# Joins, loads, an activation, two sums and the last store set at other places in a fused attention and MLP kernel

## The chip, the cores and the metric

The kernel runs on one core of one Trainium2 chip. The metric is device microseconds of one execution; before the change the median of three runs is 606.25 us (605.91 to 606.29). Lower is better.

## The reference

Two blocks follow each other. The first is a linear attention with a decaying state, for 4 batches of 8 heads, 768 tokens, head size 48; the second an MLP of 384 to 2048 to 384 on the 3072 tokens, gated with the error function of softplus.

```python
for t in range(S):
    kt, vt, rt, wt = (k[:, :, t], v[:, :, t], r[:, :, t], w[:, :, t])
    cur = np.einsum('bhd,bhe->bhde', u[None] * kt, vt)
    y[:, :, t] = np.einsum('bhd,bhde->bhe', rt, state + cur)
    state = wt[:, :, :, None] * state + np.einsum('bhd,bhe->bhde', kt, vt)
...
h = x @ w_in
sp = np.maximum(h, 0.0) + np.log1p(np.exp(-np.abs(h)))
g = h * erf(sp)
return (g @ w_out).astype(np.float32)
```

The MLP weights are given in float64. The kernel reads them as pairs of 32-bit words and makes float32 of them on the chip.

## The kernel before

**Steps.** The work is cut into 12 steps (n_steps): a chunk of 128 tokens of two of the four batches each. Step s does the attention of its chunk, and beside it the hidden layer (`hidden`, L963) of step s-1 and the output projection (`project`, L1013, from step 3 on `project_fast`, L1089) of step s-3. What runs when is written out by hand: each engine executes its instructions in the order of the program (`tc.manual_schedule`), and generators (`hidden`, `project`, `prepare`) are advanced piece by piece from `attend`.

**Attention, steps 1 to 4 (`attend`, L853).** A chunk is treated in blocks of doubling length, levels 1 to 6 (LOG). A level has products on TensorE (`level_products`, L527, into the PSUM tiles pp), a scaling of the r and k tile `in` in place on VectorE (`scale`, L302, L325), and a copy of the products that count into the tile `own` (`take_level`, L543: a masked copy, L547, or on ScalarE, L554). Step 0 (`attend_first`, L728) has an order of its own. After each level `attend` calls `early(level - 1)` ahead of the masked copy, `next(following)` behind it, and then `place(level - 1)`, which sends stages of the weight conversion (`convert_at`), activations (`advance`) and pieces of hidden layer or projection (`beside`). At the end, `through_state` (L583) adds what the state carries and copies the result to `xT`; in step 0 the last part of it is a function, `hop`, called inside step 1's first level.

**Step preparation (`prepare`, L351).** For the next step it makes the products of decay factors on GpSimd (L399). Steps from 4 on get their first 3 or 4 levels another way, the near products: terms for each distance between tokens (`term`, L457, on VectorE for short and on GpSimd for long distances), summed by VectorE (`sum_up`, L448, L450). Terms share two tiles: those of distances 0 and 4 are overwritten by those from 9 on. From step 4's preparation of step 5 on, distances go up to 15.

**Weight conversion (`convert`, L213).** The weights come in 16 pairs of column groups: 0 to 7 of w_in, 8 to 15 of w_out. A pair passes the stages l (load of its words, 2 transfers of 384 KB on SyncE's queue, three buffers), b (high word scaled on ScalarE, L245 or L247), r (low word scaled on ScalarE, L253, two buffers shared with the row loads), and j (join): h on VectorE (L262, for w_out also L267) and o, an integer addition on GpSimd (L275). The table CONVERT (L1222) says for steps 1 to 3 which stages are sent at which level; of each entry the first string is sent by `early`, the second by `place`. Before, pair 13's join is sent at level 1 of step 3, pair 14's at level 2 and pair 15's at level 3, each in the second string. The hidden layer of step 0 uses pairs 0 to 7 one by one during step 1 (one piece a level), its projection uses pairs 8 to 15 during step 3 (two pieces a level).

**Loads.** All transfers in question are issued by SyncE, in program order, and a transfer that waits holds up those behind it. `load(i, behind=x)` first copies one element of x into the buffer's first element, so the transfer waits for x. In step 0 pairs 2, 3 and 4 are loaded behind `own`; `load_step(2)` and `load_v(2)` follow in step 1 at level 2. The v transfer waits until the state products of step 0 (`pending`, L827) have been done.

**Activations.** A hidden half of 8 column groups is copied from PSUM (L1005), and then passes softplus (L978), erf (L981), each with a table load on ScalarE, and a multiplication on VectorE (L985). The list STAGES (L1229) says how many of these `advance` sends at each level of steps 1 to 3.

**The end.** `project_fast` makes the two 128-row outputs o of a step from seven products of half width. In the last step its last part (L1127 to L1132) is split into the right half (hi) and the left half (lo): the right half is added and stored ahead of the product for the left half.

Of the kernel before, what the change touches and what calls it, by code (L numbers as in the profile page):

```python
# [11 lines left out]
FP32 = mybir.dt.float32  # L12
# [5 lines left out]
P = 128  # L18
# [4 lines left out]
NJ = 2  # L23
# [16 lines left out]
DIRECT = 4  # L40
NEAR_LOG = 4
NEAR = 1 << NEAR_LOG
LOG = 6
# [18 lines left out]
def kernel(  # L62
# [14 lines left out]
    nc = tc.nc  # L77
# [8 lines left out]
    KT = DM // P  # L86
# [81 lines left out]
    def load_second(behind):  # L168
# [6 lines left out]
        load_halves(t, rkw[1])  # L175

    def load_v(s):

        vt = loaded[s][1]
        nc.sync.dma_start(out=vt[:], in_=v[s])  # L180

    def load_step(s):
        t = ins.tile([P, 2, JP, C], FP32, name="in")
        vt = ins.tile([P, NH, D], FP32, name="v")
        if s < DIRECT:
            load_halves(t, rkw[s])
        else:
            nc.sync.dma_start(out=t[:], in_=rkw[s][:, 0:2])
        if 2 < s <= DIRECT:
            load_w(s)  # L190
        if s == 3:
            nc.sync.dma_start(out=block_sb[:], in_=block_mask)
            nc.sync.dma_start(out=u_row[:], in_=u_rows)
        loaded[s] = t, vt
        if s > 2:
            load_v(s)

# [15 lines left out]
    def convert(weights):  # L213
# [6 lines left out]

        def load(i, behind=None):
            if i >= len(weights):
                return
            dst, src = weights[i]
            if plain:
                nc.sync.dma_start(out=dst, in_=src)
                return
            words = wide.tile([P, 2, DM, 2], I32, name="words", bufs=3)
            if behind is not None:
                nc.gpsimd.tensor_copy(out=words[:, 0, 0, 0:1].bitcast(FP32), in_=behind)  # L230
            load_halves(words[:].rearrange("p i n two -> p i (n two)"), src.bitcast(I32))
            held[i] = {"words": words}
# [118 lines left out]
    def prepare(s):  # L351
# [123 lines left out]
        else:  # L475
# [4 lines left out]
            term(nc.gpsimd, 5, 6, 7, 8)  # L480
            nc.vector.tensor_mul(terms[0], terms[0], r)
            sum_up(0, 4)
            term(nc.gpsimd, *range(9, NEAR))
# [99 lines left out]
    def through_state(s, xT):  # L583
# [20 lines left out]
        if not s:  # L604
            parts = y[:, 0, :, 0], y[:, 0, :, 1], y[:, 1, :, 0]

            def hop():
# [6 lines left out]
                for kk in range(KT):  # L614
                    nc.scalar.copy(by_kk[kk], parts[kk])

            turns["hop"] = hop
# [110 lines left out]
    def attend_first(xT):  # L728
# [76 lines left out]
        stages["l"](2, own[:, 0, HC // 2 : HC // 2 + 1])  # L805
        stages["l"](3)
        stages["b"](1, 0)
# [7 lines left out]
        stages["r"](1)  # L815
        stages["l"](4)
        stages["h"](1)
# [35 lines left out]
    def attend(s, xT, early, place, behind):  # L853
# [11 lines left out]
        for level in range(near_log(s) + 1 if s == DIRECT else 1, LOG + 1):  # L865
# [14 lines left out]
            if s == 1 and level == 2:  # L880
                turns.pop("pending")()
                load_step(2)
                load_v(2)
            if s != 1 or level < LOG:
# [6 lines left out]
            else:  # L891
                take_level(own, pp, level)
            if level > 1 and (s, level) != (DIRECT, LOG - 1):
                next(following, None)
            if s == 2 and level == 1:
# [4 lines left out]

                turns["ahead"] = ahead
            place(level - 1)

        from_own(s, own, 1)
# [184 lines left out]
    def project_fast(s, gs):  # L1089
# [36 lines left out]
        yield  # L1126
        parts = (hi, lo) if s == n_steps - 1 else (slice(0, DM),)  # L1127
        for part in parts:
            if part is parts[-1]:
                product(m1[:, lo], a12, b21, True)  # L1130
            nc.vector.tensor_add(o[0][:, part], o[0][:, part], m1[:, part])  # L1131
            nc.sync.dma_start(out=out[i * NJ, c, :, part], in_=o[0][:, part])  # L1132
        yield
# [60 lines left out]
    def run_late(s, tokens, following=None):  # L1194
# [30 lines left out]
        (("", "jbrl"),) * 4 + (("", "jl"), ("", ""), ("", ""), ("", ""), ("", "br")),  # L1225
        (("", "jbr"), ("", "jbr"), ("", "j")),
    )
# [19 lines left out]
    with tc.manual_schedule(  # L1247
# [15 lines left out]
        for s in range(n_steps):  # L1263
# [7 lines left out]
            def place(n):  # L1271
# [7 lines left out]
                if s in ALONE:  # L1279
                    if s == 2 and not n:  # L1280

                        next(hids[0])
                        turns.pop("ahead")()
                    convert_at(n)
                    advance(STAGES[s][n])
                else:
# [129 lines left out]
```

## Time and profile before

| what | us |
|---|---|
| median of 3 runs (lowest, highest) | 606.25 (605.91, 606.29) |
| the profiled execution | 604.11 |
| its span, first to last instruction | 602.3 |
| TensorE (PE) busy, matmuls | 584.2 (97%) |
| VectorE (DVE) busy | 436.8 (73%) |
| ScalarE (ACT) busy | 361.5 (60%) |
| GpSimd (POOL) busy | 272.5 (45%) |

Times in the timeline count from the start of the span. TensorE's clock is the share of full speed that the throttle granted, 0.994 over the span. A line such as "PE a <- POOL b: 6.5, 1, 6.5" says that TensorE's instructions a waited for GpSimd's b: 6.5 us in all, once, 6.5 at the longest; "issue" stands where the profile shows nothing that was waited for. In a timeline line stand the start, the busy time, the engine, the source line, the operation, what it writes and reads, the count, and in brackets the idle time ahead of it with its releaser. The 12 steps do not look alike: step 0 ends near 29 us, step 1 near 62, step 2 near 97, step 3 near 158, step 4 near 208, and from there a step takes 44.5 us, in which TensorE is hardly ever idle.

### The profile page before, as it was taken

The page shows a single profiled execution, that of the slowest core. Times are in us where ns is not written, and L with a number is a line of the kernel's source. Part 1 is how long each engine was busy: PE and PEld are TensorE (multiplying, and loading weights), DVE is VectorE, ACT ScalarE, POOL GpSimd, SP SyncE. Part 2 cuts the span into 40 slices and gives each one's busy share as a digit, 9 for nine tenths or more (in the row PEclk, how much of TensorE's full clock was granted, in tenths as well). Part 3 has the DMA queues.
Part 4 walks back from the last instruction along what each step waited for, and adds up shares of the span by engine and source line. Part 5 has one row for each costly group of instructions (what it writes and reads, how often), then busy time and mean ns, then how long its engine had stood idle before and what let it go on. Part 6 is the DMA issues. An engine that isn't in the chain of part 4 may idle for free.

```text
span 602.3 us, 16616 instructions
## 1 busy us (share of the span) xinstructions
PE 584.2 (97%) x7264; PEld 500.6 (83%) x7264; DVE 436.8 (73%) x519; ACT 361.5 (60%) x473; POOL 272.5 (45%) x305
## 2 busy tenths in 40 slices
PE   8889999969999999999999999999999999999997
PEld 6678787548758857899899898898898898898996
DVE  6666884979897699799799799799799624023140
ACT  4548867607435298675864765765765664746710
POOL 3546382520569739829639539549549100000000
PEclk9999999979999999999999999999999999999999
DMA  7964572313224334324334334333331300000000
GB/s 238 315 220 162 207 252 81 139 55 104 67 90 153 73 102 159 80 103 170 71 106 168 71 106 167 72 106 132 72 106 53 72 8 27 2 21 13 2 28 26
DMA packets 54081, 63.24 MB, mean 105 GB/s; under 512 B 35160, under 2 KB 40568, under 8 KB 52984
## 3 DMA queue, kind: packets, MB, share of 16 engines
q1 hardware_dynamic: 53624, 61.98, 32.3%
q8 instruction: 57, 0.93, 0.6%
q10 hardware_dynamic: 384, 0.20, 0.1%
q14 instruction: 16, 0.13, 0.1%
HBM read 52.39 MB, written 8.69 MB: 101 GB/s over the span
## 4 chain that ended last, share of the span: by engine, by line
PE 81%; DVE 8%; ACT 6%; issue 3%; POOL 1%; ACTq 1%; DVEq 0%; POOLq 0%
PE m L996 39%; PE m L1104 27%; PE pp L535 5%; PE m L1028 3%; PE y L569 2%; PE pp L641 2%; DVE in L325 1%; PE y L595 1%; PE m L839 1%; DVE words L464 1%; DVE rk L460 1%; DVE h L985 1%; ACT room L952 1%; PE pp L907 1%; DVE own L547 1%
## 5 line engine op out<-in xcount | busy, mean ns | idle before, releaser
L996 PE MATMUL m<-xT,w_in_sb 128*128 128x256 f32 x1152 | 256.7, 381 | 1.2 <-ACT h L1005 1.2
L996 PEld LDWEIGHTS m<-xT,w_in_sb 128*128 128x128 f32 x1152 | 216.3, 190 | 31.8 <-ACT h L1005 1.3
L1005 ACT COPY h<-m 128x512 f32<-128x512 f32 x96 | 55.5, 579 | 85.9 <-PE m L996 85.8
L325 DVE TENSOR_TENSOR in<-in,tot_sb 128x1024 f32<-128x1024 f32 (+1 forms) x59 | 79.7, 1351 | 25.1 <-PE pp L535 22.1
L460 POOL TENSOR_TENSOR rk<-words 128x528 f32<-128x528 f32 (+3 forms) x28 | 41.6, 1487 | 91.7 <-DVE sums L450 81.3
L464 POOL TENSOR_TENSOR words<-words,rest 128x528 f32<-128x528 f32 (+10 forms) x77 | 79.0, 1026 | 6.0
L1028 PE MATMUL m<-w_out_sb,h 128*128 128x384 f32 x192 | 66.5, 502 | 6.5 <-POOL w_out_sb L275 6.5
L1028 PEld LDWEIGHTS m<-w_out_sb,h 128*128 128x128 f32 x192 | 36.6, 195 | 31.4 <-POOL w_out_sb L275 7.1
L1104 PE MATMUL m<-w_out_sb,h 128*128 128x192 f32 x288 | 50.4, 329 | 1.0 <-DVE o L1131 1.0
L1104 PE MATMUL m<-mixed,h 128*128 128x192 f32 x288 | 51.1, 331 | 0.0
L1104 PEld LDWEIGHTS m<-w_out_sb,h 128*128 128x128 f32 x288 | 46.9, 190 | 1.8 <-DVE o L1131 1.3
L952 ACT ACT_TABLE_LOAD x36 | 46.2, 1283 | 2.7 <-issue 2.1
L1104 PEld LDWEIGHTS m<-mixed,h 128*128 128x128 f32 x288 | 46.6, 190 | 0.9
L956 ACT ACT_TABLE_LOAD x36 | 46.2, 1283 | 1.6 <-DVE room L1087 1.1
L1104 PE MATMUL m<-w_out_sb,room 128*128 128x192 f32 x256 | 44.2, 326 | 0.0
L535 PEld LDWEIGHTS pp<-in 48*64 48x64 f32 (+1 forms) x2368 | 33.5, 126 | 11.7 <-issue 6.7
L1104 PEld LDWEIGHTS m<-w_out_sb,room 128*128 128x128 f32 x256 | 42.0, 190 | 0.0
L961 DVE TENSOR_TENSOR h<-h,y 128x1024 f32<-128x1024 f32 x17 | 20.7, 1215 | 28.3 <-ACT y L956 28.2
L535 PE MATMUL pp<-in 48*64 48x64 f32 (+1 forms) x2368 | 38.0, 212 | 1.2 <-DVE in L325 1.1
L952 ACT ACTIVATE room<-h 128x1024 f32<-128x1024 f32 x36 | 38.1, 1057 | 0.4
L961 DVE TENSOR_TENSOR h<-h,pp 128x1024 f32<-128x1024 f32 x19 | 23.1, 1214 | 19.6 <-ACT pp L956 19.6
L460 POOL TENSOR_TENSOR words<-words 128x336 f32<-128x336 f32 (+6 forms) x49 | 35.3, 720 | 3.8
(140 smaller groups left out, 820.8 us busy)
## 6 DMA issues: line engine op xcount, KB each, us to landing
in<-in_rkw SPq DMA_DIRECT2D x8, 1024.0 KB, 5.4
words<-in_moe_w_in SPq DMA_DIRECT2D x16, 384.0 KB, 5.1
words<-in_moe_w_out SPq DMA_DIRECT2D x16, 384.0 KB, 4.0
words<-in_rk_rows SPq DMA_DIRECT2D x8, 768.0 KB, 5.9
w<-in_rkw SPq DMA_DIRECT2D x11, 512.0 KB, 6.6
v<-in_v SPq DMA_DIRECT2D x12, 384.0 KB, 5.8
out<-o SPq DMA_DIRECT2D x23, 192.0 KB, 2.7
in<-in_rkw SPq DMA_DIRECT2D x7, 512.0 KB, 6.1
```

What stands on the lines that cost most here:

```text
L325: nc.vector.tensor_mul(halves, halves, view(tots[level - 1], 0, [[1, n], [2, nb], [0, half]]))
L460: engine.tensor_mul(terms[n], r[:, :, n:], k[:, :, : near - n])
L464: engine.tensor_mul(k[:, :, :m], k[:, :, :m], w[:, :, n : n + m])
L535: nc.tensor.matmul(pp[s0 : s0 + m, e, n, :m], lhsT=rk[rows(e), 1, n, s0 : s0 + m], rhs=rk[rows(e), 0, n, t0 : t0 + m], start=True, stop=True,)
L569: nc.tensor.matmul(y[at(e, p), e, j, p // 2, t], lhsT=vt[t, n * NE + e, :], rhs=own[t, e * JP + n, :], start=swap == 1 and not j and not q ...
L952: nc.scalar.activation(sp_room, chunks[0], AF.Softplus)
L956: nc.scalar.activation(at, sp_room, AF.Erf)
L961: nc.vector.tensor_mul(h, h, at)
L996: nc.tensor.matmul(ps[:, ff, :], lhsT=w_in_sb[:, g * FG + f + ff, kk * P : (kk + 1) * P], rhs=xT[:, kk, :], start=kk == 0, stop=kk == KT - 1,)
L1005: nc.scalar.copy(h[:, f : f + FT, :], ps[:])
L1028: nc.tensor.matmul(ps[j][:], lhsT=gs[g][:, f, j * C : (j + 1) * C], rhs=w_out_sb[:, g * FG + f, :], start=g + f == 0, stop=g == NG - 1 and ...
L1104: nc.tensor.matmul(to, lhsT=a[:, f], rhs=b[:, f], start=start and f == 0, stop=f == FG - 1, skip_group_check=True,)
```

## The change

- CONVERT, step 3: pairs 14 and 15 are joined by `early`, ahead of the masked copies of levels 2 and 3, and so ahead of the near products of step 4 that follow these. GpSimd's addition for pair 14 comes ahead of step 4's decay products.
- Pairs 3 and 4 are no longer loaded in step 0. Their loads are sent by `hop`; pair 3's waits for the last copy to xT, by a one-element copy on ScalarE.
- Step 2's input: `load_third` makes the tiles and loads v at level 2 of step 1; the r and k halves are loaded after `place` of that level, behind pair 5.
- At level 1 of step 2, `beside` comes ahead of `advance`. In the compiled order this puts one copy L1005 ahead of the table load and the erf (L981); the softplus stays where it was.
- In `prepare` for step 5 a yield is put ahead of `sum_up(0, 4)`, and `attend` no longer leaves out `next(following)` at level 5 of step 4. The two sums (L450) follow that level's masked copy.
- The last step's last output is added and stored as a whole, after its last product.

TensorE's instructions keep their order. The diff:

```diff
--- before.py
+++ after.py
@@ -174,6 +174,12 @@
         nc.scalar.copy(t[:, 0, 0, 0:1], behind)
         load_halves(t, rkw[1])
 
+    def load_third():
+        t = ins.tile([P, 2, JP, C], FP32, name="in")
+        vt = ins.tile([P, NH, D], FP32, name="v")
+        loaded[2] = t, vt
+        load_v(2)
+
     def load_v(s):
 
         vt = loaded[s][1]
@@ -186,14 +192,13 @@
             load_halves(t, rkw[s])
         else:
             nc.sync.dma_start(out=t[:], in_=rkw[s][:, 0:2])
-        if 2 < s <= DIRECT:
+        if s <= DIRECT:
             load_w(s)
         if s == 3:
             nc.sync.dma_start(out=block_sb[:], in_=block_mask)
             nc.sync.dma_start(out=u_row[:], in_=u_rows)
         loaded[s] = t, vt
-        if s > 2:
-            load_v(s)
+        load_v(s)
 
     def near_log(s):
         return NEAR_LOG - (s == DIRECT)
@@ -218,7 +223,7 @@
         plain = weights[0][1].dtype == FP32
         signed = len(weights) // 2
 
-        def load(i, behind=None):
+        def load(i, behind=None, by_scalar=False):
             if i >= len(weights):
                 return
             dst, src = weights[i]
@@ -227,7 +232,11 @@
                 return
             words = wide.tile([P, 2, DM, 2], I32, name="words", bufs=3)
             if behind is not None:
-                nc.gpsimd.tensor_copy(out=words[:, 0, 0, 0:1].bitcast(FP32), in_=behind)
+                to = words[:, 0, 0, 0:1].bitcast(FP32)
+                if by_scalar:
+                    nc.scalar.copy(to, behind)
+                else:
+                    nc.gpsimd.tensor_copy(out=to, in_=behind)
             load_halves(words[:].rearrange("p i n two -> p i (n two)"), src.bitcast(I32))
             held[i] = {"words": words}
 
@@ -479,6 +488,8 @@
             sum_up(1, 2, 3)
             term(nc.gpsimd, 5, 6, 7, 8)
             nc.vector.tensor_mul(terms[0], terms[0], r)
+            if s == DIRECT + 1:
+                yield
             sum_up(0, 4)
             term(nc.gpsimd, *range(9, NEAR))
         yield
@@ -613,6 +624,8 @@
                     )
                 for kk in range(KT):
                     nc.scalar.copy(by_kk[kk], parts[kk])
+                stages["l"](3, xT[:, KT - 1, 0:1], True)
+                stages["l"](4)
 
             turns["hop"] = hop
             return
@@ -803,7 +816,6 @@
                 ps[:, 0].rearrange("p (n e) d -> p e n d", e=NE)[..., :D],
             )
         stages["l"](2, own[:, 0, HC // 2 : HC // 2 + 1])
-        stages["l"](3)
         stages["b"](1, 0)
         stages["b"](1, 1)
         fence()
@@ -813,7 +825,6 @@
         nc.scalar.copy(middle[rows(1)], ps[0][1][rows(1), :, :D])
         nc.vector.tensor_copy(middle[rows(0)], ps[0][0][rows(0), :, :D])
         stages["r"](1)
-        stages["l"](4)
         stages["h"](1)
         stages["h"](1)
         wait_for(HC - 1)
@@ -879,8 +890,7 @@
             scale(s, level)
             if s == 1 and level == 2:
                 turns.pop("pending")()
-                load_step(2)
-                load_v(2)
+                load_third()
             if s != 1 or level < LOG:
                 early(level - 1)
             got = pp[:].rearrange("p e n t -> p (e n) t")
@@ -890,7 +900,7 @@
                 )
             else:
                 take_level(own, pp, level)
-            if level > 1 and (s, level) != (DIRECT, LOG - 1):
+            if level > 1:
                 next(following, None)
             if s == 2 and level == 1:
 
@@ -900,6 +910,8 @@
 
                 turns["ahead"] = ahead
             place(level - 1)
+            if s == 1 and level == 2:
+                load_halves(loaded[2][0], rkw[2])
 
         from_own(s, own, 1)
         ps = products([P, JP, P])
@@ -1124,12 +1136,9 @@
         nc.vector.tensor_add(halves, halves, m0[:, None, lo].to_broadcast([P, 2, ND]))
         nc.sync.dma_start(out=out[i * NJ + 1, c], in_=o[1][:])
         yield
-        parts = (hi, lo) if s == n_steps - 1 else (slice(0, DM),)
-        for part in parts:
-            if part is parts[-1]:
-                product(m1[:, lo], a12, b21, True)
-            nc.vector.tensor_add(o[0][:, part], o[0][:, part], m1[:, part])
-            nc.sync.dma_start(out=out[i * NJ, c, :, part], in_=o[0][:, part])
+        product(m1[:, lo], a12, b21, True)
+        nc.vector.tensor_add(o[0][:], o[0][:], m1[:])
+        nc.sync.dma_start(out=out[i * NJ, c], in_=o[0][:])
         yield
 
     xTs, hids, projs = {}, {}, {}
@@ -1223,7 +1232,7 @@
         (),
         (("j", "br"),) + (("j", "brl"),) * 4 + (("j", "l"), ("", ""), ("", ""), ("", "brl")),
         (("", "jbrl"),) * 4 + (("", "jl"), ("", ""), ("", ""), ("", ""), ("", "br")),
-        (("", "jbr"), ("", "jbr"), ("", "j")),
+        (("", "jbr"), ("j", "br"), ("j", "")),
     )
 
     STAGES = {
@@ -1282,6 +1291,10 @@
                         next(hids[0])
                         turns.pop("ahead")()
                     convert_at(n)
+                    if s == 2 and not n:
+                        beside(s, next(places))
+                        advance(STAGES[s][n])
+                        return
                     advance(STAGES[s][n])
                 else:
                     advance(STAGES[s][n])
```

## The prediction

> **What bounds the kernel now.** I read the page's first part, then TensorE's waits, then the timeline around each wait. TensorE is busy 97% of the span, so what can be won is its idle time, 602.3 - 584.2 = 18.1 us, and time in which it is busy but slow. Its waits (us in total, times, longest):
>
> ```profile
> PE 584.2 (97%) x7264; PEld 500.6 (83%) x7264; DVE 436.8 (73%) x519; ACT 361.5 (60%) x473; POOL 272.5 (45%) x305
> ```
>
> ```profile
> PE m L1028 <- POOL w_out_sb L275: 6.5, 1, 6.5
> PE pp L535 <- issue: 2.9, 1, 2.9
> PE m L839 <- POOL ident masks.py:199: 1.7, 1, 1.7
> PE m L996 <- ACT h L1005: 1.2, 1, 1.2
> PE pp L535 <- DVE in L325: 1.1, 4, 0.3
> PE m L1104 <- DVE o L1131: 1.0, 1, 1.0
> ```
>
> Five of the six are touched by an edit. The largest, in step 3: projection 0 stands until GpSimd has added the last pair's low part.
>
> ```profile
> 121.94 0.95 DVE L267 SCALAR_TENSOR_TENSOR w_out_sb<-words,y 128x768 int32<-128x768 int32 x1
> 123.04 2.65 POOL L275 TENSOR_TENSOR w_out_sb<-w_out_sb,rest 128x768 int32<-128x768 int32 x1 [7.16 <-DVE w_out_sb L267]
> 125.74 6.01 PE L1028 MATMUL m<-w_out_sb,h 128*128 128x384 f32 x12 [6.47 <-POOL w_out_sb L275]
> ```
>
> The 12 matmuls after it take 6.01 us where 16 took 5.43 at 111.27, so 12 should take 4.07: a second cost, 1.94 us. The windows (length, five busy times with counts, PE clock, DMA share, GB/s) show it as clock: 0.77 in the wait, 0.52 for 4 us after it.
>
> ```profile
> 28.80:31.70 2.90, 0.04 (x3) 0.00 (x0) 0.96 (x1) 2.68 (x6) 2.74 (x4) 1.00 0.98 352
> 34.00:38.00 4.00, 4.00 (x107) 3.43 (x106) 1.60 (x2) 0.58 (x1) 0.19 (x1) 1.00 0.07 24
> 119.30:125.70 6.40, 0.00 (x0) 0.00 (x0) 6.30 (x8) 0.74 (x1) 2.66 (x2) 0.77 0.00 0
> 125.70:129.70 4.00, 3.96 (x7) 2.22 (x8) 3.79 (x8) 0.48 (x1) 1.10 (x1) 0.52 0.02 4
> ```
>
> The second wait, at 28.84, has no releaser ("issue"). In it the DMA engines are 0.98 busy, and 0.07 busy soon after. The DMA view by windows has no packet of the instruction queue q8 from 23 to 29 us; the one between 29 and 30 is
>
> ```profile
> q8 instruction: 1, 0.02, 6.1%
> ```
>
> and TensorE goes on at 31.72. So I read it as instructions that came late, behind weights (issued from 22.85) and the step-2 load (27.50). The other three waits:
>
> ```profile
> 71.63 1.91 ACT L981 ACTIVATE room<-room 128x2048 f32<-128x2048 f32 x1
> 73.45 0.56 ACT L1005 COPY h<-m 128x512 f32<-128x512 f32 x1
> ...
> 177.05 0.76 PE L535 MATMUL pp<-in 48*32 48x32 f32 x64 [0.33 <-DVE in L325]
> ...
> 596.39 2.87 PE L1104 MATMUL m<-w_out_sb,h 128*128 128x192 f32 x16 [0.97 <-DVE o L1131]
> ```
>
> ScalarE's erf (with its table, 3.2 us) stands ahead of the copy that frees TensorE's PSUM tile; a scale behind sums; and the last product behind an add that reads the other half of the same PSUM tile.
>
> [...] the 6.5 us wait was followed by 4 us at 0.52, the 2.9 us wait by none. [...] the 6 us without a q8 packet, in DMA engines 0.95 busy from 24 us on, speak for it. No run here settles this, and rival 1 keeps the doubt.
>
> **A. Loads of pairs 3 and 4 and of step 2.** A ScalarE copy (0.19 us as L174's) is added behind xT, whose copies end at 29.53; pairs 3 and 4 (1.5 MB) wait for it. SyncE stands there with pair 4 and the step-2 v behind it, which waits for TensorE's state products anyway (37.03). The step-2 input (1 MB) goes behind pair 5. [...] only pair 2 is in flight, and the stall goes. What is late next is xT: the first hidden tile can start at 29.75, not 32.33: 2.58 us. Against it: pair 3 is issued at 29.7 and lands at about 34 (4.3 us, as pair 0's halves, issued from 7.53, had landed by 11.8); it is needed by 35.3 to keep VectorE's join on time. Up to 6.6 us (as pair 5 now, issued by 38, landed by 44.7) would cost 1. Later, from 30.8 on, five pairs, v and the step-2 input, 5.4 MB at the 298 GB/s of 40 to 48 us, end at 48.9; pair 7 is wanted at 51.46 - 2.6 = 48.9, pair 6 at 48.64 - 2.6 = 46.0 and offered at 46.2 at best. I count half a microsecond for ScalarE's waits there. I take **2.0**, bounds 0.5 and 2.6.
>
> **B. Activation behind a piece.** The order of the compiled instructions shows that it is the erf (L981), not the softplus, that moves, behind one copy L1005. The copy then runs at 70.3, right after the low part at 69.39, and TensorE's wait of 1.16 goes. Behind erf nothing changes for pair 10 (74.1 against 73.91), but pair 11 waits for its DMA until 78.69 in both, and the PSUM copy behind it at 80.4 then stops a tile that would start at 80.8 by 0.3 or so: **0.75**, bounds 0.3 and 1.2.
>
> **C. Joins.** Two instructions each (0.95 + 0.95) go ahead of the masked copies of levels 2 and 3; GpSimd's adds follow. Worked forward in the times of before: pair 14's base is ready at 106.83, so VectorE joins it from 107.0 to 108.9, and GpSimd adds it until 111.6, ahead of the six totals of step 4 (4.9 us, then until 116.5; wanted only by the scales at 140). The masked copy and the gate multiply (1.33, then 1.56 for its first half) end at 111.8, where TensorE wanted that half at 111.27: it loses 0.6. Pair 15: the base at 111.8, the joining after scale 3 from 114.5 to 116.4, the add until 119.2. TensorE, 0.6 later, wants it at 119.9. So neither wait nor slow clock is left there: 6.5 + 1.9 - 0.6 = 7.8 us, until something else is late. That is VectorE: near products (6.2 us, now behind both joins) end at 123.3 and scale 4 at 124.5, while TensorE is ready at 124.0: gain 131.69 - 124.8 = 6.9. VectorE now has no idle time where it had 3.07 at 132.92 and 1.92 at 152.09; its scale in step 4 comes at 155.1 instead of 160.64 (5.5), TensorE's products at 151.8 instead of 158.64 (6.8).
>
> **D. Two sums behind the masked copy.** In step 4, 1.62 us (L450 x2, 173.49) leave VectorE's way to the level-5 scale; today that hides behind TensorE up to 0.33. After C it is VectorE that is late: 155.1 + (175.02 - 160.64) - 1.62 + up to 1.98 = 169.9 for its end, products at 170.3, a gain of 177.05 - 170.3 = 6.75. Without D it would be 5.2. GpSimd's term 9 waits for these sums, but runs at 186 behind eight others, so their new place near 172 is hidden; uncovered it would cost 1.6. C and D together: **6.75**, bounds 4.8 and 8.4 (all of wait and slow clock). From step 5 on TensorE has next to no idle time, so it is kept.
>
> **E. The last output in one piece.** The final product no longer waits for an add on its tile: 0.97 earlier. The last add is 0.56 (L1124) instead of 0.35, the last transfer 192 KB instead of 96, some 0.2 more [...]: **0.55**, bounds 0.2 and 0.9.
>
> **Sum.** 2.0 + 0.75 + 6.75 + 0.55 = 10.05 us, from the profiled 604.11 to 594.1. The median of the runs shown is 606.25, 2.1 above that execution; the same step from it gives **596.2**. Bounds: 5.8 to 13.1 us.
>
> **Rivals.** (1) The fetch stall stays or moves: pair 5, v, the step-2 input and pair 6 now pile up at 35 to 39 as pairs 2 to 4 did. For it: same bytes, same queue. Against: from 68 to 80 us the DMA engines are as full without such a stall[...]. A gives 0: 598.2. (2) VectorE takes the bound in steps 3 and 4, near products slowed by GpSimd's adds beside them (L467 takes 1.97 there, 0.95 at 162.53): C and D give 4, the sum 7.3: 599.0. For it: my margins there are under 1 us; against: VectorE has 7.0 us of waits between 104 and 177 that can absorb it. (3) Slower: the stall of (1) repeats. [...] Gains without A are 8.05 and A's own stall returns as one of these, so from four stalls on (3 x 2.9 = 8.7 lost beyond the old one) the kernel is slower; five give 606.25 - 8.05 + 4 x 2.9 = 609.8. [...] That the change doesn't do what it says is excluded by the compiled order, but for the name of the activation.
>
> **Chances.** Forecast 0.70 (own range 593.2 to 598.2), rival 1 0.10, rival 2 0.16, rival 3 0.04. Both milder rivals lie below 600, so the range is 593.2 to 600.2. Within 0.2% (1.2 us, about what a measurement of this kernel can tell from no change) needs rivals 1 and 2 together and each at its worst: 0.03. Faster 0.93, slower 0.04.
>
> **What would show it.** A: no wait "issue" near 28.8, first hidden tile near 29.8, idle DMA at 27. B: no wait of TensorE on L1005's copy. C: the last L275 near 119 less A and B, no wait on it, clock 1.00 throughout. D: level 6 of step 4 some 6.8 us earlier than A and B alone give. E: the last 16 matmuls without a gap. Wrong would be: an "issue" wait or ScalarE waits on words of over 2 us in step 1, or VectorE far behind TensorE at level 5 of step 3.

## The result and the profile after

| | before | after |
|---|---|---|
| median (lowest, highest) | 606.27 (605.91, 607.54), 4 runs | 596.56 (595.75, 598.04), 4 runs |
| ratio of the times | | 0.9839, interval 0.9815 to 0.9863 |
| the profiled execution | 604.11 | 598.04 |
| its span | 602.3 | 596.3 |
| TensorE's clock over its span | 0.994 | 0.997 |

The kernel is 9.7 us faster; the forecast was 10.05 us and 596.2. The two traces differ by only 6.1 us: the profiled execution of before is 2.2 us shorter than the median of its runs, that of after is the longest of its four. Three of those four kept a clock of 1.000; the profiled one did not, and that will matter below.

The page's first part and TensorE's waits (us in total, times, longest) of the kernel after. Lines are shifted: L275, L325, L535, L981, L996, L1005, L1028 and L1104 of before are L284, L334, L546, L993, L1008, L1017, L1040 and L1116 here.

```profile
PE 583.9 (98%) x7264; PEld 500.8 (84%) x7264; DVE 440.3 (74%) x518; ACT 361.2 (61%) x474; POOL 272.0 (46%) x305
```

```profile
PE pp L546 <- DVE in L334: 3.1, 4, 2.3
PE m L850 <- POOL ident masks.py:199: 1.7, 1, 1.7
PE m L1008 <- ACT h L1017: 1.4, 2, 1.1
PE m L1040 <- DVE h L997: 0.8, 1, 0.8
PE pp L654 <- issue: 0.6, 1, 0.6
```

Three of the five waits that the edits aimed at are gone altogether: 6.5 us for the join, 2.9 us "issue", 1.0 us at the end. Two have changed: the wait for VectorE's scale has one of 2.3 us where none was over 0.3, and the wait for the PSUM copy is still there, 1.1 us at its longest. The places, in the timeline of after:

```profile
25.33 0.61 PE L654 MATMUL pp<-v,kT 64*48 64x48 f32 x19 [0.61 <-issue]
29.40 0.69 PE L546 MATMUL pp<-rk 48*64 48x64 f32 x32
30.02 2.86 PE L1008 MATMUL m<-xT,w_in_sb 128*128 128x256 f32 x12
...
70.71 1.91 ACT L993 ACTIVATE room<-room 128x2048 f32<-128x2048 f32 x1
71.26 2.86 PE L1008 MATMUL m<-xT,w_in_sb 128*128 128x256 f32 x12
77.92 0.91 ACT L256 ACTIVATE y<-words 128x768 f32<-128x768 f32 x1 [3.22 <-DMA words<-in_moe_w_out]
80.17 2.86 PE L1008 MATMUL m<-xT,w_in_sb 128*128 128x256 f32 x12 [1.08 <-ACT h L1017]
...
116.24 1.81 POOL L284 TENSOR_TENSOR w_out_sb<-w_out_sb,rest 128x768 int32<-128x768 int32 x1 [0.76 <-DVE w_out_sb L276]
117.27 5.43 PE L1040 MATMUL m<-w_out_sb,h 128*128 128x384 f32 x16
123.76 1.22 DVE L334 TENSOR_TENSOR in<-in,tot_sb 128x1024 f32<-128x1024 f32 x1
125.03 1.16 PE L546 MATMUL pp<-in 48*64 48x64 f32 x64 [2.34 <-DVE in L334]
126.12 7.13 PE L1008 MATMUL m<-xT,w_in_sb 128*128 128x256 f32 x24
...
589.85 2.76 PE L1116 MATMUL m<-w_out_sb,h 128*128 128x192 f32 x16
592.70 0.55 DVE L1140 TENSOR_TENSOR o<-o,m 128x384 f32<-128x384 f32 x1 [2.05 <-PE m L1116]
```

From top to bottom: the second half of step 1's first level and the first hidden tile follow each other without a stall (A); the tile at 71.26 does not wait for the erf any more, but the one at 80.17 waits behind pair 11's words (B); pair 15's add ends at 118.05 and the 16 products of projection 0 run without a gap (C); then VectorE's scale is late, and the tile behind it takes 7.13 us where 24 such products take 5.45 elsewhere. The last 16 products come without a gap (E). The windows of after (length, busy times of PE, PEld, DVE, ACT, POOL with counts, PE clock, DMA share, GB/s):

```profile
26.00:28.00 2.00, 1.66 (x94) 1.40 (x85) 2.00 (x4) 1.79 (x3) 1.31 (x2) 1.00 0.37 143
28.00:30.00 2.00, 2.00 (x38) 1.52 (x38) 0.60 (x1) 0.49 (x2) 2.00 (x2) 1.00 0.00 0
122.69:125.03 2.34, 0.01 (x1) 0.00 (x1) 2.31 (x4) 0.48 (x1) 0.00 (x0) 1.00 0.43 112
125.03:129.03 4.00, 4.00 (x72) 3.43 (x73) 3.79 (x9) 0.00 (x0) 0.00 (x0) 0.70 0.91 340
```

The DMA engines, 0.98 busy in the old stall, are empty from 28 to 30 us. What the prediction named as a sign of being wrong did come up in step 1: ScalarE waits 2.75 us for pair 3's words, until 35.02. That is inside the 35.3 that the prediction had worked out as still in time, and TensorE does not wait there; before has a wait of 2.87 us of the same kind, for a later pair. Behind the wait for VectorE the clock averages 0.70 for 4 us.

Since TensorE's instructions have one order in all these kernels, its n-th product can be compared between traces. Starts in us, with the kernels of the next section beside them (C+D is the stretch in which those two act: the difference of the third and fifth row; each trace is one execution, and the one without B is already 1.0 us later than after at the first hidden tile, before B acts):

| TensorE's | before | after | without B | terms late | terms late, loads late |
|---|---|---|---|---|---|
| first hidden tile of step 1 | 32.33 | 30.02 | 31.04 | 29.43 | 29.80 |
| second hidden tile of step 2 | 66.26 | 64.41 | 64.98 | 63.86 | 64.27 |
| first projection product, step 3 | 98.37 | 97.10 | 97.82 | 98.63 | 97.12 |
| level 5 of step 3 | 131.69 | 125.03 | 125.54 | 124.12 | 122.40 |
| level 6 of step 4 | 177.05 | 171.68 | 170.50 | 171.26 | 169.56 |
| C+D: from row 3 to row 5 | 78.68 | 74.58 | 72.68 | 72.63 | 72.44 |
| first product of the last step's outputs | 561.46 | 556.04 | 554.78 | 555.91 | 553.80 |

### The profile page after: what moved, and what is told of

The parts are those of the page before. It is cut to its first block, busy times and chain, and to the rows that moved or that the text cites. A ratio compares the mean times of both kernels' runs of the same rounds, so it can differ in the third digit from the quotient of the medians.

```text
span 596.3 us, 16614 instructions
## 1 busy us (share of the span) xinstructions
PE 583.9 (98%) x7264; PEld 500.8 (84%) x7264; DVE 440.3 (74%) x518; ACT 361.2 (61%) x474; POOL 272.0 (46%) x305
## 4 chain that ended last, share of the span: by engine, by line
PE 88%; DVE 5%; ACT 3%; DMA 1%; issue 1%; ACTq 0%; POOL 0%; DVEq 0%; SPq 0%; POOLq 0%
PE m L1008 39%; PE m L1116 28%; PE m L1040 8%; PE pp L546 5%; PE y L580 2%; PE pp L654 2%; DVE in L334 2%; PE y L606 2%; DMA words<-in_moe_w_out 1%; PE m L850 1%; PE pp L919 1%; DVE h L997 1%; ACT rest L262 1%; DVE own L558 1%; ACT y L256 1%
## 5 line engine op out<-in xcount | busy, mean ns | idle before, releaser
L1008 PE MATMUL m<-xT,w_in_sb 128*128 128x256 f32 x1152 | 258.6, 383 | 1.5 <-ACT h L1017 1.4
L1008 PEld LDWEIGHTS m<-xT,w_in_sb 128*128 128x128 f32 x1152 | 217.4, 191 | 33.1 <-ACT h L1017 1.6
L1017 ACT COPY h<-m 128x512 f32<-128x512 f32 x96 | 55.5, 580 | 87.5 <-PE m L1008 87.4
L334 DVE TENSOR_TENSOR in<-in,tot_sb 128x1024 f32<-128x1024 f32 (+1 forms) x59 | 82.6, 1400 | 16.4 <-PE pp L546 14.3
L469 POOL TENSOR_TENSOR rk<-words 128x528 f32<-128x528 f32 (+3 forms) x28 | 42.4, 1514 | 91.6 <-DVE sums L459 81.2
L1040 PE MATMUL m<-w_out_sb,h 128*128 128x384 f32 x192 | 64.3, 491 | 0.8 <-DVE h L997 0.8
L1040 PEld LDWEIGHTS m<-w_out_sb,h 128*128 128x128 f32 x192 | 35.7, 190 | 24.5 <-issue 0.9
L1116 PE MATMUL m<-mixed,h 128*128 128x192 f32 x288 | 51.1, 331 | 0.0
L1116 PE MATMUL m<-w_out_sb,h 128*128 128x192 f32 x288 | 50.3, 329 | 0.0
L1116 PEld LDWEIGHTS m<-w_out_sb,h 128*128 128x128 f32 x288 | 46.9, 190 | 0.5
L1116 PEld LDWEIGHTS m<-mixed,h 128*128 128x128 f32 x288 | 46.6, 190 | 0.9
L546 PEld LDWEIGHTS pp<-in 48*64 48x64 f32 (+1 forms) x2368 | 33.4, 126 | 13.6 <-DVE in L334 6.0
L1116 PE MATMUL m<-w_out_sb,room 128*128 128x192 f32 x256 | 44.2, 326 | 0.0
L1116 PEld LDWEIGHTS m<-w_out_sb,room 128*128 128x128 f32 x256 | 42.0, 190 | 0.0
L546 PE MATMUL pp<-in 48*64 48x64 f32 (+1 forms) x2368 | 37.7, 212 | 3.1 <-DVE in L334 3.1
L469 POOL TENSOR_TENSOR words<-words 128x336 f32<-128x336 f32 (+6 forms) x49 | 35.3, 720 | 3.8
```

What stands on the lines that cost most here:

```text
L334: nc.vector.tensor_mul(halves, halves, view(tots[level - 1], 0, [[1, n], [2, nb], [0, half]]))
L469: engine.tensor_mul(terms[n], r[:, :, n:], k[:, :, : near - n])
L546: nc.tensor.matmul(pp[s0 : s0 + m, e, n, :m], lhsT=rk[rows(e), 1, n, s0 : s0 + m], rhs=rk[rows(e), 0, n, t0 : t0 + m], start=True, stop=True,)
L1008: nc.tensor.matmul(ps[:, ff, :], lhsT=w_in_sb[:, g * FG + f + ff, kk * P : (kk + 1) * P], rhs=xT[:, kk, :], start=kk == 0, stop=kk == KT - 1,)
L1017: nc.scalar.copy(h[:, f : f + FT, :], ps[:])
L1040: nc.tensor.matmul(ps[j][:], lhsT=gs[g][:, f, j * C : (j + 1) * C], rhs=w_out_sb[:, g * FG + f, :], start=g + f == 0, stop=g == NG - 1 and ...
```

## The experiments

Theories. T1: the prediction's, that A ends a wait for a late packet of instructions, B ends a wait that pair 11's words limit again, and C and D go until VectorE is late. Rivals: the packet is held by something else than the weights that were moved; B is worth nothing; what stops C and D is the single wait at level 5 of step 3 and not VectorE's amount of work. All ratios are to the kernel before, run on the same chip in between.

**One part alone, one part left out.** `a_only` is before with A's edits; `no_a`, `no_b` and `no_d` are after without A's, B's and D's. The edits of B and D, as they are undone:

```diff
-                    if s == 2 and not n:
-                        beside(s, next(places))
-                        advance(STAGES[s][n])
-                        return
...
-            if s == DIRECT + 1:
-                yield
             sum_up(0, 4)
...
-            if level > 1:
+            if level > 1 and (s, level) != (DIRECT, LOG - 1):
```

A's edits, as `a_only` adds them and `no_a` undoes them (with load_third and load's third parameter, shown in the change):

```diff
+                stages["l"](3, xT[:, KT - 1, 0:1], True)
+                stages["l"](4)
...
-        stages["l"](3)
...
-        stages["l"](4)
...
+            if s == 1 and level == 2:
+                load_halves(loaded[2][0], rkw[2])
```

> Only the loads of pairs 3 and 4 and of step 2's input are moved (part A); the rest is as before. Theory 1, the prediction's: the stall of 2.9 us at 28.8 was TensorE waiting for instructions behind the loads, so it is gone or under 1 us, the first hidden tile starts near 30.0, and since the later stalls stay as they are, some 1.3 to 2.0 us of it last: 604.3 to 605.0 where before is 606.3. Theory 2, the stall is a property of the program and not of the loads: it stays near 2.9 us, and the time is that of before. Theory 3, the late landing of pair 11 in step 2 sets the time of step 2 whatever happens ahead: step 3 starts (first L1028) no more than 0.8 us earlier than 98.4.

Measured: 604.02 (602.62 to 605.35), ratio 0.9965 (0.9951 to 0.998): 1.9 us below the kernel before as run beside it (605.89). The "issue" stall is gone.

> The whole change without part A. Theory 1: the stall of 2.9 us near 28.8 is back, step 1 ends about 1.5 us later than in the changed kernel, and if nothing later absorbs it the time is 597.9 to 598.6 (changed kernel 596.6). Theory 3 (pair 11's words set step 2): step 3 starts at the same time as in the changed kernel within 0.5 us, and the time is that of the changed kernel.

Measured: 600.82 (597.44 to 602.99), ratio 0.9903 (0.9876 to 0.993). The stall is back:

```profile
29.59 0.34 PE L537 MATMUL pp<-rk 48*64 48x64 f32 x6
31.98 0.67 PE L537 MATMUL pp<-rk 48*64 48x64 f32 x26 [2.05 <-issue]
```

It is 4.3 us slower than after at the median, 1.7 at the lowest run. Its profiled execution, with a clock of 0.994 over its span, also has TensorE wait 1.70 us for a small transfer to xT, and the products behind it are slow: 20 take 6.19 us where they take 4.55 in the fastest kernel below, behind a wait of 1.75 for the same transfer.

```profile
69.12 6.19 PE L998 MATMUL m<-xT,w_in_sb 128*128 128x256 f32 x20 [1.70 <-DMA xT<-y]
```

Wait and slow products are 3.3 us, and this kernel starts step 3 at 101.07 where after does at 97.10. So most of what its trace shows as lost is not the old stall. Such waits appear in two other traces (2.03 us in `c_only`, without A, and 1.75), and in neither of the main ones.

> The whole change without part B (erf ahead of the piece again). Theory 1, the prediction's 0.75 us for B: TensorE waits 1.2 us for ScalarE's copy near 72, step 3 starts 0.7 us later and the time is 597.3. Theory 3: the wait near 72 is back, but pair 11 lands when it lands, so TensorE waits less near 80 (1.1 and 0.3 us in the changed kernel), and step 3 starts within 0.3 us of the changed kernel's 97.1: time as the changed kernel.

Measured: 596.93 (596.52 to 599.52), ratio 0.9856 (0.9834 to 0.9878): 0.4 us more than after (1.0 us by the two ratios), with overlapping intervals. In the traces, from the second hidden tile of step 2 to step 3, it takes 32.84 us without B and 32.69 with it: 0.15. In place, B gains next to nothing.

> The whole change without part D (the two sums ahead of the scale again). Theory 1, the prediction's 1.5 us for D once C is in: in step 4 the scale of level 5 ends near 172.5 and the products of level 6 start near 172.7 instead of 171.7, and the time is 598.1. Theory 4: VectorE was less late than predicted (in the changed kernel the scale ended at 170.7 and the products started at 171.7, one us of slack), so only 0.3 to 0.7 us are lost, below what the times can tell: 597.0.

Measured: 597.48 (596.17 to 597.88), ratio 0.9852 (0.9834 to 0.9871): 0.9 us more than after, again with overlapping intervals.

**Which half of A?** `a_pairs` adds only the first two lines above to before and drops the two old loads; `a_in` adds only load_third and the late load_halves.

> The kernel before, with one half of A: the words of pairs 3 and 4 are loaded behind xT; step 2's input stays where it was. If the packet of instructions that comes late is held by the weight words issued from 22.85 on, the stall of TensorE near 28.8 is gone (under 0.3 us of 'issue' there) and the first hidden tile follows the second half of level 1 by under 1.1 us, at 604.0, as A alone gave. If it is step 2's input (1 MB, issued at 27.5) that holds it, the stall of 2 to 3 us stays and the time is that of the kernel before, 605.9.

> The kernel before, with the other half of A: step 2's r and k halves are loaded behind pair 5; pairs 2 to 4 are loaded in step 0 as before. If the words of pairs 2 to 4 hold the packet, a stall of 2 to 3 us stays near 28.8 and the time is that of the kernel before, 605.9 within 1. If step 2's input holds it, the stall is gone, at 604.0.

Measured: 604.27 (602.12 to 608.34, 22 runs), ratio 0.9975 (0.9961 to 0.999), for the pairs; 605.97 (603.55 to 609.45, 14 runs), ratio 1.0001 (0.9986 to 1.0016), for the input. The words of pairs 3 and 4 are what counts, and moving the input gains nothing that can be measured in the times. The input may still lengthen the stall: in the trace of `a_in`, the shortest of its 14 runs, 1.24 us are left of it, less than the 2 to 3 expected, with the DMA engines full:

```profile
29.03 0.34 PE L540 MATMUL pp<-rk 48*64 48x64 f32 x6
30.60 0.67 PE L540 MATMUL pp<-rk 48*64 48x64 f32 x26 [1.24 <-issue]
```

```profile
28.00:30.00 2.00, 1.36 (x12) 0.82 (x10) 0.24 (x1) 0.87 (x3) 2.00 (x2) 1.00 0.99 360
```

The instruction queue q8 tells the same: after a packet between 22 and 23 us in all four kernels, the next comes between 29 and 30 us in before, 28 and 29 in `a_in`, but 26 and 27 in `a_pairs` and in after. From 24 to 29 us the DMA engines are 0.96 and 0.93 busy in the first two, 0.47 and 0.51 in the last two. Its share of a window of 1 us, in after from 26 to 27:

```profile
q8 instruction: 1, 0.02, 6.0%
```

In the trace of `a_pairs` the stall near 28.8 is gone too, but the first hidden tile comes only at 31.41. A wait of 0.91 us ("issue") ended at 25.30 there, and from 26 to 28 us the clock was 0.73, from 28 to 30 it was 0.50; the six products take 2.54 us where they take 1.56 in after:

```profile
28.32 2.54 PE L613 MATMUL y<-y,mixed 128*128 128x256 f32 x6
28.00:30.00 2.00, 2.00 (x19) 1.61 (x13) 0.58 (x1) 0.00 (x0) 2.00 (x2) 0.50 0.00 0
```

**C alone.**

```diff
-        (("", "jbr"), ("", "jbr"), ("", "j")),
+        (("", "jbr"), ("j", "br"), ("j", "")),
```

> The kernel before with the joins of pairs 14 and 15 moved, and nothing else. The prediction gave C alone 5.2 us by the end of level 5 of step 4, thus 600.7. If the two kernels with and without the other edits are right that VectorE is late at level 5 of step 3 for 2.3 us and the clock then drops in some executions, it is 4.3 (clock drops) to 6.0 (it does not): 601.6 to 599.9. TensorE's interval from step 3's first projection product to level 5 of step 3 is 27.8 (33.3 before) either way; the clock of the tile behind that wait tells them apart.

Measured: 601.49 (600.21 to 604.59), ratio 0.9933 (0.9912 to 0.9954): 4.5 us. The profiled execution is the longest of six. Its clock is 0.992 over the span, and its products are slow three times: behind the old stall (2.33 us; 11 products of the first hidden tile take 4.04 us, where all 12 take 2.86 in after), behind a wait of 2.03 us for the transfer to xT (the first four take 1.85 us, where four took 1.13 at 67.54), and behind the wait for VectorE (clock 0.59 from 132 to 134 us). Only the last has to do with C:

```profile
130.72 1.16 PE L535 MATMUL pp<-in 48*64 48x64 f32 x64 [2.34 <-DVE in L325]
131.82 7.13 PE L996 MATMUL m<-xT,w_in_sb 128*128 128x256 f32 x24
```

The wait of 2.34 us is to the digit that of after, without A, B and D: it comes from C.

**Pair 11's words earlier.** In after, the transfers of w, block mask, u and v for step 3 are issued between those of its r and k and pair 11's. This kernel puts them behind pair 11.

```diff
             load_halves(t, rkw[s])
+            if s == 3:
+                loaded[s] = t, vt
+                return
...
-        if s == 3:
-            nc.sync.dma_start(out=block_sb[:], in_=block_mask)
-            nc.sync.dma_start(out=u_row[:], in_=u_rows)
...
+    def load_rest(s):
+        load_w(s)
+        nc.sync.dma_start(out=block_sb[:], in_=block_mask)
+        nc.sync.dma_start(out=u_row[:], in_=u_rows)
+        load_v(s)
...
                     if s == 2 and not n:
+                        load_rest(3)
                         beside(s, next(places))
```

> The changed kernel, in which the row loads w of step 3, the block mask, u and v of step 3 are issued behind the load of pair 11 and no longer ahead of it. If what B wins is given back because pair 11's words come late (ScalarE waited 3.2 us for them at 77.9, then TensorE 1.1 for the copy behind them), ScalarE's wait shrinks by 1 us or more, TensorE's 1.1 goes, step 3's first projection product comes at 95.6 instead of 97.1, and the time is 595.1. If the DMA engines are simply full there, what is issued later comes late in its turn (w or the r and k of step 3): no gain, 596.6.

Measured: 597.62 (596.37 to 597.67), ratio 0.986 (0.9845 to 0.9875): not faster, and yet its first half went as expected. Pair 11 is no longer waited for (ScalarE now waits 1.37 us for pair 12, which holds up nothing), the five tiles of step 2 run without a wait of over 0.3 us, and step 3's first projection product comes at 95.09. Of the 2.0 us won, 1.4 were lost again 25 us later, behind the same wait of 2.34 us, where the clock now stayed low for 6 us:

```profile
120.46:122.80 2.34, 0.00 (x1) 0.01 (x1) 2.31 (x4) 0.48 (x1) 0.00 (x0) 0.95 0.48 114
122.80:128.80 6.00, 6.00 (x74) 5.08 (x75) 5.79 (x12) 0.00 (x0) 0.00 (x0) 0.50 0.73 275
```

The same wait in the kernel without B left the clock alone:

```profile
123.20:125.54 2.34, 0.00 (x1) 0.00 (x1) 2.31 (x4) 0.48 (x1) 0.00 (x0) 1.00 0.34 103
125.54:129.54 4.00, 4.00 (x77) 3.60 (x78) 3.79 (x9) 0.02 (x1) 0.00 (x0) 1.00 1.00 364
```

**The near products' terms later.** This takes away what makes TensorE wait at level 5 of step 3.

```diff
-            term(nc.vector, 1, 2, 3)
+            term(nc.vector, 1)
             yield
-            term(nc.vector, 4, 5, 6, 7)
-            nc.vector.tensor_mul(terms[0], terms[0], r)
-            yield
+            term(nc.vector, 2, 3, 4)
+            yield
+            term(nc.vector, 5, 6, 7)
+            nc.vector.tensor_mul(terms[0], terms[0], r)
             sum_up(*range(near))
```

> The changed kernel, in which only the first of the near products' terms (distance 1, with distance 0) stands ahead of level 4's scale in step 3; distances 2 to 4 follow level 4's masked copy, distances 5 to 7 and the sums level 5's. VectorE's work stays the same. If VectorE's lateness at level 5 of step 3 is what C lacks, TensorE's wait of 2.3 us there goes (2.6 us of terms moved), its clock stays at 1.00 in the tile behind it, and the time is 2.3 to 4 us shorter than that of the changed kernel: 594.2 to 592.5. If VectorE, busy without a gap from 104 on, is late one or two levels on instead, a wait of about 2 us stands at level 6 of step 3 or in step 4, and the time is 596.5.

Measured: 596.68 (595.6 to 597.9), ratio 0.9838 (0.9807 to 0.9868): not faster than after. The theory of the one wait falls. The wait is gone and the clock behind it is 1.00, but TensorE arrives earlier at a VectorE that is not done earlier; it now waits at level 6 of step 4:

```profile
122.48 1.22 DVE L334 TENSOR_TENSOR in<-in,tot_sb 128x1024 f32<-128x1024 f32 x1
124.12 1.16 PE L547 MATMUL pp<-in 48*64 48x64 f32 x64
125.21 5.45 PE L1009 MATMUL m<-xT,w_in_sb 128*128 128x256 f32 x24
...
168.89 2.32 DVE L334 TENSOR_TENSOR in<-in,tot_sb 128x1024 f32<-128x1024 f32 x1
171.26 0.76 PE L547 MATMUL pp<-in 48*32 48x32 f32 x64 [0.98 <-DVE in L334]
```

The C+D row of the table says it shortest: 72.63 us with the terms late, 72.68 in the kernel without B, which has the wait of 2.34 us at level 5 and a clock of 1.00. With the clock up, the wait is not what counts. What is left is the amount of work, VectorE's above all; in after it is busy 41.4 of the 42 us from 104 to 146:

```profile
104.00:146.00 42.00, 38.88 (x416) 28.22 (x414) 41.38 (x45) 22.53 (x23) 11.32 (x10) 0.96 0.32 111
```

In the fastest kernel below, VectorE is busy 63.9 and TensorE 63.6 of the 66.0 us from 103.57 to level 6 of step 4, so little is left to win there by moving waits.

The profiled execution lost time at another place: its wait for pair 11 was 1.90 us, and there too the clock fell (0.57 over the next 4 us), for a tile of 4.54 us instead of 2.86. Three of its six runs kept a clock of 1.000 and took 595.6 to 596.0, three had 0.997 and took 597.4 to 597.9.

```profile
78.19 0.86 ACT L256 ACTIVATE y<-words 128x768 f32<-128x768 f32 x1 [4.30 <-DMA words<-in_moe_w_out]
80.39 4.54 PE L1009 MATMUL m<-xT,w_in_sb 128*128 128x256 f32 x12 [1.90 <-ACT h L1018]
```

**Both.** The last two edits together take away the two waits behind which the clock fell in after and in the kernel with the terms late.

> The same with the loads of step 3 behind pair 11's as in the run that showed pair 11 less late. There the 2 us won by 98 us were lost again in the slow clock behind the wait at level 5 (7.75 and 1.99 us where 5.38 and 1.08 are usual). If that is why it was not faster, with the wait gone the gain shows: 2 us less than the kernel with the terms moved alone, 592.2 to 590.5. If the loads only move the lateness on, the two are the same within 0.5 us.

Measured: 594.98 (594.7 to 595.8), ratio 0.9809 (0.9778 to 0.984). All six runs kept 0.999 or 1.000. It is 1.7 us below the kernel with the terms late, but only 0.8 below those three runs of it that kept the clock. Its trace, the longest of the six runs, has the wait of 1.75 us for xT; the clock of that execution is 1.000, and the 20 products behind the wait take the 4.55 us given above. It beats after by 1.6 us at the median, less than the 4.4 us or more that were expected; the runs of the two hardly touch (594.7 to 595.8 against 595.75 to 598.04), though the intervals of the ratios overlap. It was the fastest kernel of all.

**B and D where less hides them.** The two undoings from above, made to that kernel.

> That kernel without B: at level 1 of step 2 the erf stands ahead of the copy again. With pair 11 less late, B's lead should no longer be given back: this kernel is 1.2 us (TensorE's wait behind the erf) to 2.8 us slower than the one with B, and TensorE has a wait of 1.2 us on the copy near 73. If B is worth nothing whatever the loads do, the two are the same within 0.5 us.

Measured: 596.69 (595.58 to 597.86), ratio 0.9838 (0.9807 to 0.9868): 1.7 us more than with B at the median, between the 1.2 and 2.8 expected. But its runs fall into two groups of three, 595.6 to 595.8 and 597.5 to 597.9, and the first is only 0.7 above the median with B. The trace is of the first group; what the others lost is in no trace. The wait behind the erf is back:

```profile
69.61 1.91 ACT L1000 ACTIVATE room<-room 128x2048 f32<-128x2048 f32 x1
71.43 0.57 ACT L1024 COPY h<-m 128x512 f32<-128x512 f32 x1
72.05 2.86 PE L1015 MATMUL m<-xT,w_in_sb 128*128 128x256 f32 x12 [1.11 <-ACT h L1024]
```

> The best kernel so far (near products' terms moved, step 3's loads behind pair 11) without D: the two sums stand ahead of level 5's scale of step 4 again. In that kernel TensorE waits 0.97 us for this scale at level 6 of step 4, so VectorE sets the time there. If so, the two sums (1.6 us) now count almost whole: less 0.3 us for the scale, which ran in 2.3 us beside GpSimd and in 2.0 us later, TensorE's wait at level 6 grows from 0.97 to 2.3 us and the time to 596.2. If VectorE is not what bounds step 4 and D is worth 0.4, as between the kernels with and without D at the old place of the terms, it is 595.4.

Measured: 598.15 (596.23 to 599.82), ratio 0.9878 (0.9853 to 0.9903): 3.2 us more than with D at the median, where 1.2 was expected. The one run with a clock of 1.000 took 596.23, which is the time expected. The wait is the 2.3 us that were expected:

```profile
168.43 1.61 DVE L465 TENSOR_REDUCE sums<-words 128x16 f32<-128x768 f32 x2
169.96 1.97 DVE L340 TENSOR_TENSOR in<-in,tot_sb 128x1024 f32<-128x1024 f32 x1
171.99 0.76 PE L551 MATMUL pp<-in 48*32 48x32 f32 x64 [2.27 <-DVE in L340]
```

From step 3's first projection product to level 6 of step 4 it takes 74.28 us, 1.84 more than with D: 1.3 in this wait, and 0.6 earlier, in one for the gate's multiplication in step 3, which D does not touch. So the traces give D 1.3 us. This execution also has pair 3's words late in step 1: ScalarE waits 5.73 us for them, until 38.26, and TensorE 1.72 behind it. That is the risk that the prediction counted under A; in no other trace of this case does pair 3 hold TensorE for more than 0.2 us. The clock of this execution is 0.999, and 1.00 from 172 to 178 us, behind the wait of 2.27; four of the six runs have 0.991 or 0.997, so in others it probably fell. That would be the rest of the 3.2 us, but no trace shows it.

## Why the prediction was right, and where it was not

**A, 2.0: right where it stands alone.** Alone it measured 1.9 us. The first hidden tile came at 30.02 against "29.75", and the half microsecond counted for step 1 was 0.46 (66.26 - 32.33 = 33.93 us to step 2's second tile before, 64.41 - 30.02 = 34.39 after). Of rival 1, that the stall stays or moves, nothing came: the 0.6 us at 25.33 stand in the trace without A as well (0.6). The reading of the stall without a releaser as late instructions is borne out: loading other words later moved the packet and the stall together. Why one queue's backlog delays another's packet is not shown; what was measured is that in before a packet came 6 us or more after the one before (none from 23 to 29 us), behind the words of pairs 2 to 4 (2.3 MB). That leaving A out costs 4.3 us at the median, where A alone gains 1.9, is for its profiled execution mostly the wait of 1.70 us for xT and the slow products behind it. Since such waits come with A as well, they cannot be put down to A; the runs of that kernel spread over 5.6 us, and how often the wait comes is not known.

**B, 0.75: the mechanism right, but not in a sum with A.** The wait of 1.16 us went. The prediction has that "pair 11 waits for its DMA until 78.69 in both", and the copy behind it then stops a tile "by 0.3 or so": pair 11 came at 77.92, so just 0.77 us of the lead of A and B could pass, and the tile behind it waited 1.08 us instead of 0.3. The prediction held pair 11's time fixed and yet added A's 2.0 and B's 0.75 in full. Both leads end at pair 11: together they brought step 3 forward by 1.27 us (98.37 to 97.10), where 2.75 were expected. In place B is worth 0.4 at the median; with pair 11's words earlier, 0.7 to 1.7.

**C and D, 6.75: mis-sized.** C's joins went as worked out: the add ended at 118.05 (119.2 less the 1.27 us of A and B is 117.9), TensorE was ready for level 5 at 122.69 (124.0 less 1.27 is 122.73), and the loss of 0.6 at the first half was 0.8. The step that failed is "near products (6.2 us, now behind both joins) end at 123.3 and scale 4 at 124.5": less 1.27 that is 123.2, and it was 124.98. They began 0.8 us later and took 7.15 us. The 6.2 already held 1.97 for the first of them, beside a GpSimd addition. In after the first (L476) took 2.26, and the second (L469) 1.49 instead of 0.85, beside the GpSimd product (L926) that now follows the addition. In step 4, with GpSimd idle, the same two sizes take 0.95 (at 157.57) and 0.86 (at 160.31). So the wait was 2.34 us instead of 0.8. This is rival 2's mechanism, VectorE slowed beside GpSimd. It is read from what ran at the same time; no run takes GpSimd's work away. In the profiled execution the stretch C+D is 4.1 us shorter than before, the 4 that rival 2 named, but 1.7 of what is missing is the slow clock; with the clock up it is 6.0 shorter (78.68 - 72.68).

"Clock 1.00 throughout" failed in that execution: 1.7 us (7.07 us from that tile's start to the next group's instead of 5.38). The prediction had the wait of 2.9 us in before, with no slow clock behind it, and took shorter waits to cost nothing there: its author's estimate. Here waits of 2.34 us and less were followed by a slow clock in some executions (0.70 over 4 us in this one).

**D: alone 0.33 at most, with C 1.5 (6.75 less 5.2).** In after it was worth 0.4 us in the traces (38.89 against 38.49 us from level 6 of step 3 to level 6 of step 4) and 0.9 at the median. It was TensorE, held back at level 5, that came late to level 6: the scale there ended at 170.72, the products began at 171.68. Once TensorE came on time, D's 1.3 us showed in the wait.

**E, 0.55: right.** From the first product of the last step's outputs to the end of the span it is 602.3 - 561.46 = 40.84 us before, 596.3 - 556.04 = 40.26 after: 0.58. The 0.2 us counted for the larger last transfer was an estimate; from the end of the last add to the end of the span it is 2.66 us in before (96 KB) and 3.05 in after (192 KB).

**The sum** was 10.05 and the result 9.7, and that they lie so near is in part luck. The sum was worked out on the profiled execution of before, 604.11. From trace to trace A and B gave 1.27 us, C and D 4.1, E 0.6: 6.0, or 7.7 without the slow clock. The three runs of after that kept the clock, 595.75 to 596.75, lie 7.4 to 8.4 below 604.11. The rest of the 9.7 is that the median of before lies 2.2 us above its profiled execution; no run shows what those 2.2 us are. The parts as measured one by one (A 1.9, B 0.4, C 4.5, D 0.9, E 0.6) give 8.3; with the spread of 1 to 6 us between runs of one kernel they cannot be expected to close better. Of rival 3, repeated stalls of that kind, nothing was seen: TensorE's longest "issue" wait in after is 0.6 us.

## What to carry to other kernels

When a wait is removed, work forward on every engine that shares the stretch, with durations that hold beside the neighbours it will then have: a 0.95 us instruction was 2.26 us beside another engine. A wait moved out of the way is worth its length only if the engine waited for has idle time to give; in a stretch where VectorE is busy 41.4 of 42 us, shifting its work moved the wait and not the end. And a small saving upstream shows only when what comes next is not late for another reason: in the traces D was worth 0.4 us in place and 1.3 once the waits after it were gone, and B's two values at the median are 0.4 and 1.7. For the same reason two edits that lead to one late transfer must not be added up: A and B gave 1.27 us together, not 2.75. Last, a profile is one execution: see where it lies among the runs before pricing an edit from it.

## What the runs showed of the hardware that was not expected

- Behind the wait of 2.34 us at level 5, TensorE's clock fell in five of the six traces that have it: 2 us windows behind it read as low as 0.50 in after and with pair 11 earlier, 0.52 without D, 0.53 without A and 0.59 in `c_only`, for a loss of 1.7 us (after, `c_only`) to 3.1 us (pair 11 earlier). Without B it read 1.00, and nothing was lost. The clock fell as well behind single waits of 1.90 us (terms late: 0.57 over 4 us) and 0.91 us (`a_pairs`: 0.50 from 28 to 30 us), for a loss of 1.7 us each, and the products were slow behind waits of 2.33 and 2.03 us (`c_only`) and 1.70 us (without A). It read 1.00 behind waits of 2.88 us (before, 32 to 38 us) and 2.27 us (terms and loads late, without D; 0.999 over that span, which has a wait of 1.72 us too); behind waits of 2.05 us (without A: 7 products in 1.78 us) and 1.75 us (terms and loads late: 20 in 4.55 us) the products kept their pace. So between 0.91 and 2.88 us the length of the wait did not decide here; what does is not shown. The runs of the kernel with the terms late fell into two groups, 595.6 to 596.0 and 597.4 to 597.9.
- The instruction queue q8 moved 0.93 MB in 57 packets, 16 KB each. In before and `a_in`, with the words of pairs 2 to 4 (2.3 MB) given to another queue, none came from 23 to 29 and from 23 to 28 us; in after and `a_pairs` the next came before 27. That these packets hold TensorE's instructions is a reading. The stall (2.9 us in before, 1.2 in `a_in`; 2.1 and 2.3 without A and in `c_only`) has no releaser in the profile; beside it the DMA engines were 0.98 busy in before and 0.99 in `a_in`. The small transfers to xT near 63 us differed from trace to trace: without A those on SyncE's queue took 3.6 us to land at the median, and TensorE waited 1.70 us; in before and after they took 1.7, and TensorE did not wait for them. In `c_only` and with terms and loads late it waited 2.03 and 1.75 us.
